# Spectral filter and low-rank mixer on one core: batch 0's spectra made twice by TensorE, one copy of the filters for its products, tables loaded from SP

## The chip, the core and the metric

The kernel runs on one core of one Trainium2 chip. The core has TensorE (PE; PEld is its weight load), VectorE (DVE), ScalarE (ACT), GpSimd (POOL) and SyncE (SP), each with an instruction queue of its own that it works through in order. PE writes to PSUM (eight banks of 2 KB in each of 128 partitions); DVE and ACT read PSUM and write SBUF; POOL works on SBUF. Transfers between memory and SBUF are issued from SP, ACT or POOL and share 16 DMA engines. The metric is the device time of one execution in microseconds (us), given as the median of three runs. The profile is taken from one further execution; its times are us from the start of its span.

## The reference

```python
batch, seq, dim = (8, 3136, 256)
n_freq = seq // 2 + 1
...
X = np.fft.rfft(x, axis=1)
F = (filt_r + 1j * filt_i)[None, :, :]
Y = X * F
y = np.fft.irfft(Y, n=x.shape[1], axis=1).astype(np.float32)
...
xt = y.transpose(0, 2, 1)
h = xt @ U @ V                      # U (3136, 32), V (32, 3136)
u = y + h.transpose(0, 2, 1)
ch = np.maximum(u @ w_ch1, 0.0) @ w_ch2     # 256 -> 1024 -> 256
out = (u + ch).astype(np.float32)
```

Inputs and output are float32; the kernel works in float16 with float32 sums in PSUM.

## The kernel before

The length 3136 is split as 64 x 49. A forward transform is then: a first stage of 64 points over q (matrix `w64`), a second stage of 49 points that takes in the twiddle factors (tables `t2`, one 98 x 128 matrix for each of 32 values of s), the product with the filter, and the two stages back (tables `g12`, then `s2` or `low`). A spectrum tile `px` holds, for two values of s, real parts of up to 49 frequencies in partitions 0 to 63 and imaginary parts in 64 to 127.

The filters lie in `ft`, in two halves of 32 x 256 columns. The first half holds the real parts in both partition halves; the second holds the imaginary parts in partitions 0 to 63 and, with the sign turned, in 64 to 127. So a product has two parts, `px` times the first half and `px` times the second, and the second needs `g12` with its partition halves exchanged (`swap_table`, POOL; for the first eight s a ready table `gs` is loaded). The highest frequency is put into `ft[64]` by a DVE copy from `nyq`.

**Batch 0** stays on the chip. `first_f1` makes the first stage from x (24 evacuations to `at`, half on DVE, half on ACT, with filler matmuls of `keep_on` between), `first_a` turns pieces of it with an identity matrix, and `first_mid` runs over 16 pairs of s (m): `forward` (px, one bank of tag "m"), `both_products` (one DVE instruction of 128 x 1024), `back` (8 matmuls into `pi`), and ACT's two copies into `et`. Four times, once for each eighth-of-64 part of the tables (`PARTS`), DVE first makes the second copies of the filters, `swap_real` and `swap_imag`. Fillers (`keep_in`) stand ahead of each px. Then 50 transposes give `e2`.

**Batches 1 to 7** go through memory between the stages: first-stage units (`f1_units`: one matmul of 512 columns, one copy on ACT or DVE, writes to `c1`; 13 units for a batch, from three pieces of x), `load_a`, products and the way back in `stream`, writes to `c2`, `load_e`. Batch 1 uses `both_products` and the exchanged tables, later batches `product` (three DVE instructions, one sum on POOL) and `g12`'s first half alone.

**The mixer** runs over groups of 4 x 128 columns: `make_u`, eight `mm1` with relu, `mm2` and the output. Its loop counts slots, about 48 to a batch; the work on the transforms of later batches is put into slots by hand (`put`, `run`). Unit k of batch 2's first stage is put at slot 4 + 1.1 k, which makes its first unit stand in slot 4 and the fifth, the first of the second piece of x, in slot 8.

**Queues.** POOL issues all loads of x, filters, tables, U, V and weights, in the order of the code: x of batch 0, filters and tables in four parts, x of batch 1 with `swap_table` between, V, w1, w2. Then, after `first_f1` in the code, x of batch 2 (first piece), the 14 copies of `v_order` that reorder V into `low`, x of batch 2 (second piece), and two copies that reorder w2. SP loads small constants at the start, then writes `c1` of batch 1.

PSUM's eight banks: tag "x" 1, "f" 1, "m" 4, "o" 2.

Of the kernel before, what the change touches and what calls it, by code (L numbers as in the profile page):

```python
# [13 lines left out]
SEQ = 3136  # L14
# [12 lines left out]
def _consts():  # L27
# [22 lines left out]
    for s in range(NS):  # L50
        for j in range(49):
# [15 lines left out]
            else:  # L67
# [3 lines left out]
                g[s, j, o:o + 49] = ei.real * (2 if f else 1)  # L71
                g[s, 64 + j, o:o + 49] = -ei.imag * 2

    t2[0, :, 64] = 0
    t2[0, 49:, 64] = (-1.0) ** r
    g[0, 64] = 0
    g[0, 64, 49:] = (-1.0) ** r
    g *= ESC / n
    gs = np.concatenate([g[:, 64:], g[:, :64]], 1)
# [5 lines left out]
            np.ascontiguousarray(g.reshape(4, 8, 128, 98).transpose(0, 2, 1, 3)).astype(f16),  # L85
            np.ascontiguousarray(gs[0:8].transpose(1, 0, 2)).astype(f16))
# [3 lines left out]
def kernel(  # L90
# [13 lines left out]
    w64_np, s2_np, idn_np, fold_np, wp_np, t2_np, g_np, gs_np = _consts()  # L104
# [7 lines left out]
    gs_d = nc.inline_tensor(gs_np, name="gsd")  # L112
# [8 lines left out]
    BUFS = {"x": 1, "f": 1, "m": 4, "o": 2}  # L121

    def bank(tag, name):
        return ps.tile([128, 512], F32, tag=tag, bufs=BUFS[tag], name=name)
# [48 lines left out]
    nyq = sb.tile([128, DM], F32, tag="ocho", bufs=1, name="nyq")  # L173
    PARTS = ((0, 8), (8, 16), (16, 24), (24, 32))
    for a, b in PARTS:
        for c in (0, NS * DM):
            nc.vector.memset(ft[32:64, c + a * DM:c + b * DM], 0.0)  # L177

    def load_table(k, a, b):

        dst, src, w = ((t2, t2_d, 128), (g12, g_d, 98))[k]
        n, p = (b - a) * w, dst.shape[0]
        nc.gpsimd.dma_start(dst[:, a * w:b * w],
                            bass.AP(tensor=src, offset=a // 8 * p * n, ap=[[n, p], [1, n]]))

    def swap_table(a, b):

        o = NS * 98
        for p, q in ((0, 64), (64, 0)):
            nc.gpsimd.tensor_copy(g12[p:p + 64, o + a * 98:o + b * 98],  # L190
                                  g12[q:q + 64, a * 98:b * 98])

    def load_filters(a, b):

        d = max(a, 1)
        for c, src in ((0, filt_r), (NS * DM, filt_i)):
            nc.gpsimd.dma_start(
                ft[0:24, c + a * DM:c + b * DM],
                bass.AP(tensor=src.tensor, offset=a * DM, ap=[[64 * DM, 24], [1, (b - a) * DM]]))
            nc.gpsimd.dma_start(  # L200
                ft[25:49, c + d * DM:c + b * DM].rearrange("p (k d) -> p k d", d=DM),
# [3 lines left out]
    def load_rest():  # L205

        for c, src in ((0, filt_r), (NS * DM, filt_i)):
            nc.gpsimd.dma_start(
                ft[25:49, c:c + DM],
                bass.AP(tensor=src.tensor, offset=32 * DM, ap=[[64 * DM, 24], [1, DM]]))  # L210
            nc.gpsimd.dma_start(
                ft[24:25, c:c + NS * DM],
                bass.AP(tensor=src.tensor, offset=24 * 64 * DM,
                        ap=[[NS * DM, 1], [1, NS * DM]]))
        nc.sync.dma_start(
            nyq[64:65, :],
            bass.AP(tensor=filt_r.tensor, offset=(SEQ // 2) * DM, ap=[[DM, 1], [1, DM]]))

    def swap_real(a, b):

        nc.vector.tensor_copy(ft[64:128, a * DM:b * DM], ft[0:64, a * DM:b * DM])

    def swap_imag(a, b):

        fb = NS * DM
        if a == 0:
            nc.vector.memset(ft[0:1, fb:fb + DM], 0.0)
        nc.vector.tensor_scalar_mul(ft[64:128, fb + a * DM:fb + b * DM],
                                    ft[0:64, fb + a * DM:fb + b * DM], -1.0)
# [9 lines left out]
    for k, part in enumerate(PARTS):  # L239
        if k:  # L240
            load_table(0, *part)
        load_filters(*part)
        if k == 0:
            load_table(0, *part)
        load_table(1, *part)
        if k == 0:
            nc.gpsimd.dma_start(g12[:, NS * 98:(NS + 8) * 98], gs_d.ap())
        if k > 1:
            swap_table(*PARTS[k - 1])
    load_x(1, 0)  # L250
    uq = sb.tile([128, NR * RANK], F16, tag="esb", bufs=2, name="uq")
    nc.vector.memset(uq[64:128, :], 0.0)
    nc.gpsimd.dma_start(uq[0:64, :], moe_U.rearrange("(q r) p -> q (r p)", q=NQ))
    load_x(1, 1)
    swap_table(*PARTS[3])
    load_x(1, 2)
    vqs = []
    for k in range(2):
        v = sb.tile([128, SEQ // 2], F16, tag="xt", bufs=5, name="vq")
        vqs.append(v)  # L260
        nc.gpsimd.dma_start(v[64:96, :], moe_V[:, k * (SEQ // 2):(k + 1) * (SEQ // 2)])
    w1 = cst.tile([128, 2 * 1024], F16)
    for i in range(4):
        nc.gpsimd.dma_start(
            w1[32 * i:32 * i + 32, :].rearrange("p (h c) -> p h c", h=2),
            bass.AP(tensor=moe_w_ch1.tensor, offset=moe_w_ch1.offset + i * 64 * 1024,
                    ap=[[1024, 32], [32 * 1024, 2], [1, 1024]]))
    w2 = cst.tile([128, 8 * DM], F16)
    w2n = sb.tile([128, 8 * DM], F16, tag="esb", bufs=2, name="w2n")
    nc.gpsimd.dma_start(w2n, moe_w_ch2.rearrange("(cc t) e -> cc (t e)", t=8))  # L270
# [6 lines left out]
    def v_order():  # L277

        for r in range(0, NR, 8):
# [8 lines left out]
            yield  # L288

# [66 lines left out]
    def first_f1():  # L356
        ne = 0
        xs = [st[0]["x"][c] for c in range(len(CH))]
        for r0 in range(0, NH - 1, 4):
            for dh in range(2):  # L360
                keep_on(4 if r0 < 16 else 0)
# [6 lines left out]
                for h in range(2):  # L368
                    dst = atv[:, dh, :, h * NH + r0:h * NH + r0 + 4]
                    src = pa.rearrange("p (r h k) -> p h k r", h=2, k=64)[:, h]  # L370
                    if ne % 2:
                        nc.vector.tensor_copy(dst, src)
                    else:
                        nc.scalar.copy(dst, src)
                    ne += 1
# [21 lines left out]

# [542 lines left out]
```

## Time and profile before

| | us |
|---|---|
| median of 3 runs | 523.87 |
| lowest, highest | 523.34, 524.46 |
| the profiled execution | 523.76 |
| its span | 522.0 |
| batch 0's 16 products on DVE, first start to last end | 19.98 to 44.16 |
| first `mm1` of the mixer (slot 0) | 53.61 |
| first px of batch 1 | 64.45 |

A line of the timeline has the start, the time from there to the end of the merged instructions, the engine, the source line, the operation, what it writes and reads with shapes, how many instructions are merged, and in square brackets the idle time of the engine before it and what ended it. A matmul's row is longer than the time it keeps PE, since matmuls are pipelined; the distance of starts tells the latter.

### The profile page before, as it was taken

The page shows a single profiled execution, that of the slowest core. Times are in us where ns is not written, and L with a number is a line of the kernel's source. Part 1 is how long each engine was busy: PE and PEld are TensorE (multiplying, and loading weights), DVE is VectorE, ACT ScalarE, POOL GpSimd, SP SyncE. Part 2 cuts the span into 40 slices and gives each one's busy share as a digit, 9 for nine tenths or more (in the row PEclk, how much of TensorE's full clock was granted, in tenths as well). Part 3 has the DMA queues.
Part 4 walks back from the last instruction along what each step waited for, and adds up shares of the span by engine and source line. Part 5 has one row for each costly group of instructions (what it writes and reads, how often), then busy time and mean ns, then how long its engine had stood idle before and what let it go on. Part 6 is the DMA issues. An engine that isn't in the chain of part 4 may idle for free.

```text
span 522.0 us, 11372 instructions
## 1 busy us (share of the span) xinstructions
PE 496.7 (95%) x3976; PEld 327.4 (63%) x3976; DVE 407.7 (78%) x585; ACT 377.5 (72%) x772; POOL 301.9 (58%) x430
## 2 busy tenths in 40 slices
PE   4878899999989999999999999999999999999997
PEld 3766477777656665666666666666666666555555
DVE  7897386677888888998998888988999877436654
ACT  2767757768778768887788878888777678665552
POOL 7798733445765757775777675965666564313001
PEclk9999999999999999999999999999999999999999
DMA  8989998978899798887898698888777575644325
GB/s 135 188 143 221 233 214 203 213 209 191 197 202 253 180 203 181 215 219 176 235 216 221 162 253 207 184 227 194 180 194 150 129 167 134 139 100 80 71 62 121
DMA packets 122571, 93.99 MB, mean 180 GB/s; under 512 B 58017, under 2 KB 104866, under 8 KB 122514
## 3 DMA queue, kind: packets, MB, share of 16 engines
q1 hardware_dynamic: 98986, 50.93, 39.1%
q0 software_dynamic: 20240, 40.60, 37.9%
q10 hardware_dynamic: 3288, 1.74, 1.3%
q8 instruction: 31, 0.51, 0.4%
q14 instruction: 26, 0.21, 0.1%
HBM read 56.25 MB, written 48.17 MB: 200 GB/s over the span
## 4 chain that ended last, share of the span: by engine, by line
PE 78%; DVE 9%; DMA 6%; POOL 3%; issue 2%; ACT 1%; ACTq 0%; SPq 0%; DVEq 0%; POOLq 0%
PE phh L712 28%; PE po L789 25%; PE px L516 5%; PE pi L552 5%; PE pu L637 4%; PE po L738 4%; DVE uv L537 4%; DMA xt<-in_x_dram 3%; PE pf L472 3%; PE ph L594 2%; DVE ft L177 1%; DVE uv L535 1%; DMA out_dram<-och 1%; DMA g<-gd 1%; DMA a<-c 1%
## 5 line engine op out<-in xcount | busy, mean ns | idle before, releaser
L720 ACT ACTIVATE h<-phh 128x512 f16<-128x512 f32 (+1 forms) x391 | 205.4, 578 | 68.6 <-PE phh L712 64.1
L712 PE MATMUL phh<-ut,w 128*128 128x512 f16 x768 | 197.5, 379 | 0.3 <-ACT h L720 0.3
L540 POOL TENSOR_TENSOR y<-uv 128x512 f16<-128x512 f16 x96 | 111.8, 1165 | 100.1 <-DVE uv L537 80.3
L789 PE MATMUL po<-h,w 128*128 128x512 f16 x656 | 168.5, 379 | 0.0
L712 PEld LDWEIGHTS <-w 128*128 128x128 f16 x832 | 114.2, 144 | 54.5 <-issue 0.9
L537 DVE TENSOR_TENSOR uv<-px,ft 64x512 f16<-64x512 f32 x192 | 132.1, 688 | 2.6
L807 POOL DMA_DIRECT2D out_dram<-och x148 | 85.9, 588 | 81.6 <-DVE och L799 38.9
L789 PEld LDWEIGHTS <-w 128*128 128x128 f16 x656 | 60.5, 98 | 57.8 <-issue 1.1
L535 DVE TENSOR_TENSOR uv<-px,ft 128x512 f16<-128x512 f32 x96 | 64.9, 676 | 35.2 <-PE px L516 33.0
L556 ACT CAST esb<-pi 98x512 f16<-98x512 f32 x112 | 65.9, 589 | 32.1 <-PE pi L552 28.2
L798 DVE TENSOR_TENSOR tt<-po,ut 128x512 f32<-128x512 f32 x82 | 56.7, 692 | 34.3 <-PE po L789 32.3
L799 DVE STREAM_TRANSPOSE och<-tt 128x512 f32<-128x512 f32 x82 | 58.4, 712 | 2.8
L516 PE MATMUL px<-a,t 98*128 98x256 f16 x256 | 49.1, 273 | 5.6 <-DVE uv L537 2.8
L478 ACT CAST asb<-pf 128x512 f16<-128x512 f32 (+1 forms) x80 | 46.1, 576 | 6.5 <-PE pf L472 3.8
L524 DVE TENSOR_TENSOR uv<-px,ft 128x1024 f16<-128x1024 f32 x32 | 38.0, 1219 | 11.7 <-PE px L516 11.2
L702 ACT CAST ut<-pu 128x512 f16<-128x512 f32 x82 | 44.8, 612 | 0.0
L516 PEld LDWEIGHTS <-t 98*128 98x128 f16 x256 | 22.7, 98 | 31.6 <-DVE uv L537 10.6
L552 PE MATMUL pi<-y,g 128*98 128x256 f16 x192 | 36.7, 272 | 0.1
L472 PE MATMUL pf<-xt,w 128*128 128x512 f16 (+1 forms) x91 | 33.2, 370 | 1.0 <-DMA xt<-in_x_dram 1.0
L738 PE MATMUL po<-w,h 128*128 128x256 f16 x256 | 33.2, 273 | 0.0
L552 PEld LDWEIGHTS <-g 128*98 128x98 f16 x256 | 29.6, 123 | 3.2 <-issue 0.8
L637 PEld LDWEIGHTS <-e 96*128 96x128 f16 x686 | 26.4, 98 | 7.2
(99 smaller groups left out, 420.0 us busy)
## 6 DMA issues: line engine op xcount, KB each, us to landing
xt<-in_x_dram POOLq DMA_DIRECT2D x46, 256.0 KB, 6.6
out_dram<-och SPq DMA_DIRECT2D x180, 64.0 KB
a<-c SPq DMA_DIRECT2D x28, 384.0 KB
e<-c SPq DMA_DIRECT2D x56, 192.0 KB
out_dram<-och POOLq DMA_DIRECT2D x148, 64.0 KB, 3.5
c<-esb SPq DMA_DIRECT2D x24, 384.0 KB
c<-asb POOLq DMA_DIRECT2D x30, 256.0 KB, 5.6
out_dram<-och POOLq DMA_DIRECT2D x12, 256.0 KB, 4.8
```

The source lines that it names most:

```text
L516: nc.tensor.matmul(px[:, sl * DM:(sl + 1) * DM], t2[:, s * 128:(s + 1) * 128], a2[:, (2 * ml + sl) * DM:(2 * ml + sl + 1) * DM], start=Tru ...
L535: nc.vector.tensor_mul(uv[:, 0:512], px[:, :], ft[:, a:a + 512])
L537: nc.vector.tensor_mul(uv[p:p + 64, 512:1024], px[q:q + 64, :], ft[q:q + 64, b:b + 512])
L540: nc.gpsimd.tensor_add(y, uv[:, 0:512], uv[:, 512:1024])
L552: nc.tensor.matmul(pi[0:98, sl * DM:(sl + 1) * DM], g12[:, g:g + 98], y[:, o:o + DM], start=(fi == 0), stop=(fi == nf - 1), skip_group_che ...
L556: nc.scalar.copy(split(esb[:, ml * 512:(ml + 1) * 512]), natural(pi[0:98, :]))
L712: nc.tensor.matmul(pm[:, 0:w], w1[:, dh * 1024:(dh + 1) * 1024].rearrange("p (c t) -> p t c", t=8)[:, t], ut[:, dh * w:(dh + 1) * w], star ...
L720: nc.scalar.activation(h[:, 0:w], pm[:, 0:w], RELU)
L789: nc.tensor.matmul(po[:, :], w2[:, t * DM + dh * 128:t * DM + (dh + 1) * 128], hs[gx, t][:, :], start=(t == 0), stop=(t == 7))
L798: nc.vector.tensor_add(tt, po[:, :], uts[gx][:, dh * 512:(dh + 1) * 512])
L799: nc.vector.transpose(och.rearrange("p (j h a) -> p h j a", h=2, a=32)[:, dh], tt.rearrange("p (j t) -> p j t", t=32))
L807: (nc.gpsimd if k and (b < nb - 1 or r0 > 12) else nc.sync).dma_start(dst, och[32 * i:32 * i + 32, k * 512:(k + 1) * 512] .rearrange("p (r ...
```

## The change

For batch 0, each px is made twice over: the real parts of two s, once in partitions 0 to 63 and once in 64 to 127 (first 512 columns, bank one), and likewise the imaginary parts (second bank). One DVE instruction multiplies all 1024 columns with one copy of the filters, in which partitions 0 to 63 hold real and 64 to 127 imaginary parts. The second copies that later batches need are made by 12 DVE copies (`spread_filters`): one between the middle and `prep_u`, one behind the transposes, ten in slots 0 to 9. The sign that stood in the filters moves into the exchanged table (POOL multiplies by -1) and, for batches 2 to 7, into a `scalar_tensor_tensor`. The highest frequency is handled as a 50th row of the first s, so `nyq`, `gs` and the fills of row 64 go.

Tables of parts 1 to 3 are loaded from SP, each pair behind a one-element copy (`mark`) of a tile that the queue thereby waits for. POOL's order becomes: x of batch 0, tables part 0, filters of parts 0 and 1, swap 0, filters 2, swap 1, filters 3, U, swap 2, batch 1's first two pieces of x, swap 3, its third, V, w1, w2, three steps of `v_order`, batch 2's first piece, the other four steps, w2's copies, batch 2's second piece. Batch 0's px tiles take two banks each, from a pool that uses the four banks of tag "m". In `first_f1` the evacuations go by tile and not by half tile, and the fillers are 4, 4, 4, 4, 12, 2, 2, 2; the fillers of the middle go. Batch 1's first-stage units move from the last four products to one there, one behind, and six among the transposes.

```diff
     for s in range(NS):
-        for j in range(49):
+        for j in range(49 if s else 50):
...
-    t2[0, :, 64] = 0
-    t2[0, 49:, 64] = (-1.0) ** r
-    g[0, 64] = 0
-    g[0, 64, 49:] = (-1.0) ** r
+    t2[0, :, (64, 113)] = 0
+    g[0, (64, 113)] = 0
...
+    @contextmanager
+    def four_banks(k):
+
+        with tc.tile_pool(name=f"pm{k}", bufs=2, space=bass.MemoryType.PSUM) as pool:
+            pm.append(pool)
+            yield
...
     for a, b in PARTS:
-        for c in (0, NS * DM):
-            nc.vector.memset(ft[32:64, c + a * DM:c + b * DM], 0.0)
+        for p in (32, 96):
+            nc.vector.memset(ft[p:p + 32, a * DM:b * DM], 0.0)
...
     def swap_table(a, b):
 
         o = NS * 98
-        for p, q in ((0, 64), (64, 0)):
-            nc.gpsimd.tensor_copy(g12[p:p + 64, o + a * 98:o + b * 98],
-                                  g12[q:q + 64, a * 98:b * 98])
+        nc.gpsimd.tensor_copy(g12[0:64, o + a * 98:o + b * 98], g12[64:128, a * 98:b * 98])
+        nc.gpsimd.tensor_scalar_mul(g12[64:128, o + a * 98:o + b * 98],
+                                    g12[0:64, a * 98:b * 98], -1.0)
...
+    def spread_filters():
+
+        for a, b in PARTS:
+            lo, hi = slice(a * DM, b * DM), slice((NS + a) * DM, (NS + b) * DM)
+            for dst, src in ((ft[0:64, hi], ft[64:128, lo]), (ft[64:128, hi], ft[64:128, lo]),
+                             (ft[64:128, lo], ft[0:64, lo])):
+                nc.vector.tensor_copy(dst, src)
+                yield
...
+    def tables_behind(k, ap):
+
+        nc.sync.dma_start(mark[:, k:k + 1], ap)
+        for t in range(2):
+            load_table(t, *PARTS[k], eng=nc.sync)
+
+    load_table(0, *PARTS[0])
+    load_filters(*PARTS[0])
+    load_table(1, *PARTS[0])
...
+    load_filters(*PARTS[1])
+    swap_table(*PARTS[0])
+    load_filters(*PARTS[2])
+
+    def loads(k):
+
+        swap_table(*PARTS[k])
+        if k == 1:
+            load_filters(*PARTS[3])
+            nc.gpsimd.dma_start(uq[0:64, :], moe_U.rearrange("(q r) p -> q (r p)", q=NQ))
+        elif k == 2:
+            load_x(1, 0)
+            load_x(1, 1)
+        else:
+            load_x(1, 2)
...
+    def load_weights():
...
+        for k, _ in enumerate(v_order()):
+            if k == 2:
+                load_x(2, 0)
+        for h in range(2):
+            nc.gpsimd.tensor_copy(split(w2)[:, :, h], natural(w2n)[:, :, h])
+        load_x(2, 1)
...
     def first_f1():
-                keep_on(4 if r0 < 16 else 0)
+                keep_on(4 if r0 < 8 else 12 if r0 == 8 and not dh else 2 if r0 < 16 else 0)
...
+            if r0 == 20:
+                tables_behind(1, atv[0:1, 0, 0, r0:r0 + 1])
...
     def first_a(m):
...
+        if ml == 0 and gi in (1, 2):
+            tables_behind(gi + 1, st[0]["a"][gi][0:1, 0:1])
+            loads(gi + 1)
+            if gi == 2:
+                load_weights()
...
     def first_mid(fill):
...
-        def ahead(m, keep=0):
-            return forward(m, st[0]["a"][m // 4], ("m",), keep)
-
-        pxs = [ahead(0), ahead(1)]
-        keep_on(8)
-        for m in range(NS // 2):
-            for k, part in enumerate(PARTS):
-                if k and 2 * m == part[0]:
-                    swap_real(*part)
-                    swap_imag(*part)
-            uv = both_products(m, pxs.pop(0))
-            if pend is not None:
-                back(*pend)
-            pend = (m, uv)
-            if m + 2 < NS // 2:
-                pxs.append(ahead(m + 2, 4 if m % 4 or not m else 14))
-            if m + 3 < NS // 2:
-                first_a(m + 3)
-            if m >= 12:
-                next(fill)
+        def ahead(m):
+
+            px = pm[-1].tile([128, 1024], F32, tag="px", bufs=2, name="px")
+            for fi in range(2):
+                for sl in range(2):
+                    s, o = 2 * m + sl, fi * 512 + sl * DM
+                    for q in (0, 64):
+                        nc.tensor.matmul(
+                            px[q:q + 64, o:o + DM], t2[:, s * 128 + fi * 64:s * 128 + fi * 64 + 64],
+                            st[0]["a"][m // 4][:, s % KG * DM:(s % KG + 1) * DM],
+                            start=True, stop=True, tile_position=(0, q), skip_group_check=True)
+            return px
+
+        with four_banks(1):
+            pxs = [ahead(0), ahead(1)]
+            for m in range(NS // 2):
+                uv = sb.tile([128, 1024], F16, tag="uv", bufs=3, name="uv")
+                fap = ft[:, 2 * m * DM:2 * (m + 1) * DM]
+                nc.vector.tensor_mul(
+                    uv.rearrange("p (f e) -> p f e", f=2),
+                    pxs.pop(0).rearrange("p (f e) -> p f e", f=2),
+                    bass.AP(tensor=fap.tensor, offset=fap.offset, ap=[fap.ap[0], [0, 2], [1, 512]]))
+                if pend is not None:
+                    back(*pend)
+                pend = (m, uv)
+                if m + 3 < NS // 2:
+                    first_a(m + 3)
+                if m + 2 < NS // 2:
+                    pxs.append(ahead(m + 2))
+                if m == NS // 2 - 1:
+                    next(fill)
+        later.enter_context(four_banks(2))
+        next(spread)
+        next(fill)
         prep_u()
         back(*pend)
...
-            if k4 in (1, 2, 3, 4):
+            if k4 < 6:
                 next(fill)
+            if k4 == 6:
+                next(spread)
...
     def product(m, px):
-        for p, q in ((0, 64), (64, 0)):
-            nc.vector.tensor_mul(uv[p:p + 64, 512:1024], px[q:q + 64, :],
-                                 ft[q:q + 64, b:b + 512])
+        nc.vector.scalar_tensor_tensor(uv[0:64, 512:1024], px[64:128, :], -1.0, ft[64:128, b:b + 512],
+                                       op0=mybir.AluOpType.mult, op1=mybir.AluOpType.mult)
+        nc.vector.tensor_mul(uv[64:128, 512:1024], px[0:64, :], ft[0:64, b:b + 512])
...
+    later = ctx.enter_context(ExitStack())
+    with four_banks(0):
+        first_f1()
+    loads(1)
     for m in range(3):
         first_a(m)
...
+    for k in range(10):
+        put(k, spread)
```

## The prediction, made before the changed kernel was run

> **What bounds the kernel now.** First the page's head and the busy table, then the busy time by stretches, whose first columns are the stretch, its length, and busy us (count) of PE, PEld, DVE, ACT and POOL.
>
> ```profile
> span 522.0 us, 11372 instructions
> PE 496.7 (95%) x3976; PEld 327.4 (63%) x3976; DVE 407.7 (78%) x585; ACT 377.5 (72%) x772; POOL 301.9 (58%) x430
> ...
> 20.00:44.00 24.00, 20.09 (x310) 17.34 (x307) 23.59 (x22) 16.38 (x47) 21.29 (x33) 1.00 0.92 161
> 53.60:65.00 11.40, 9.81 (x53) 5.54 (x53) 3.08 (x6) 9.30 (x19) 8.11 (x15) 1.00 1.05 242
> 110.00:480.00 370.00, 365.49 (x2806) 231.69 (x2805) 301.71 (x444) 288.32 (x585) 228.19 (x307) 1.00 0.79 186
> ```
>
> From 110 to 480 TensorE (PE) is busy 99%, so what the change moves before that reaches the end only as an earlier or later start of this stretch. In 20 to 44 (batch 0's middle) VectorE (DVE) is the full engine: 23.59 of 24.00. DVE in order of time (start, us, engine, line) shows the pattern, which repeats four times:
>
> ```profile
> 24.63 0.69 DVE L221 COPY ft<-ft 64x2048 f16<-64x2048 f16 x1
> 25.24 1.32 DVE L228 TENSOR_SCALAR ft<-ft 64x2048 f16<-64x2048 f16 x1
> 26.67 4.62 DVE L524 TENSOR_TENSOR uv<-px,ft 128x1024 f16<-128x1024 f32 x4
> ```
>
> Four products at 1.155 (4.62/4), then some 2.0 of filter copies. The 16th product ends at 44.16. Behind the middle, PE and GpSimd (POOL) in order of time show what comes last:
>
> ```profile
> 57.74 0.38 PE L472 MATMUL pf<-xt,w 128*128 128x512 f16 x1 [0.71 <-DMA xt<-in_x_dram]
> 62.78 0.39 PE L472 MATMUL pf<-xt,w 128*128 128x512 f16 x1 [0.27 <-DMA xt<-in_x_dram]
> ```
>
> ```profile
> 25.05 2.22 POOL L190 COPY g<-g 64x784 f16<-64x784 f16 x2 [0.69 <-DMA g<-gd]
> 35.84 1.71 POOL L190 COPY g<-g 64x784 f16<-64x784 f16 x2
> 47.50 8.56 POOL L284 COPY low<-vq 32x256 f16<-32x256 f16 x14
> 56.01 1.17 POOL L154 DMA_DIRECT2D xt<-in_x_dram  x2
> 57.22 2.01 POOL L837 COPY w<-w2n 128x1024 f16<-128x1024 f16 x2
> 102.10 1.15 POOL L540 TENSOR_TENSOR y<-uv 128x512 f16<-128x512 f16 x1 [2.29 <-DVE uv L537]
> ```
>
> The waits at 57.74 and 62.78 are for batch 2's first and second piece of x. The second is issued at 56.01 behind POOL's 8.56 of V reordering; its two transfers take 5.3 and 6.2 to land, the last at 62.74. So the second bound is POOL's queue: a shorter middle helps only as far as that piece lands earlier too.
>
> **The change, part by part.** Rows are us of the profiled execution.
>
> First stage: transfers of x are in the same places of POOL's queue, and the last piece of batch 0 lands at 15.2 as before. The fillers thin out: 0.107 each there (four L347 rows take 0.43). DVE and ACT each still evacuate 12 half tiles. PE's tiles from r=16 on still follow the third x piece (issued at 7.53, 7.1 to land: 14.6), so I take 0.4 less: the last ACT copy ends at 17.6 instead of 17.98. The thinner fillers have one more risk: PE's 128-column matmuls start 0.107 apart to 16.6 (L366) and 0.055 apart from 18.03 (L394). If that doubling came only after 19, each product until then would cost PE up to 1.2 more; PE is idle here for 2.0 at most (9.9 to 11.9) instead of 3.0, so I take 0.
>
> Middle, removed: four L221 (2.90), four L228 (4.02), L227 (0.17) and L828 (0.28) on DVE, 7.4 in all; on PE 86 filler matmuls at 0.055. Added on PE: px becomes eight 64-column matmuls of 256 in place of two of 128 columns. Line 594 already runs 32-column matmuls of 128 rows side by side: fours start 3 to 4 ns apart, and the fours follow at 0.11. Line 323 (64 columns) runs its two pairs in 0.35, where one 512-column matmul takes 0.21. So a pair costs 0.11, eight 0.44, against 0.22 for the old two. Going into and out of such a group costs about 0.1 each: L472 at 43.785 (0.21 long, as L712's four in 0.86) is followed by L323 at 44.095, and line 594's last start at 116.83 by L712 at 117.03. PE per product: eight L413 0.36, four L394 0.22, px 0.44, two changes 0.2, a semaphore 0.04: 1.26. The order matters: with two px buffers, px of product m+2 waits for product m, so PE's 1.26 is the period and not DVE's 1.155. First product: pt and ACT copies as at 18.03 to 19.3 before, less 0.4, plus 0.3 for the dearer px: 19.4, where before it was 19.98 (DVE's copies). End: 19.4 + 15 x 1.26 + 1.2 = 39.5, against 44.16: 4.7 gained.
>
> Behind the middle: six first-stage units of batch 1 stand among the transposes instead of four, two with fillers: 2 x (0.22 + 0.33) = 1.1, on PE, which is dense there (45.78 to 49.66). ACT's copies of two units come before its last et copies: +0.2. Left at slot 0 (L712, 53.61 before): 3.4, at 50.2.
>
> The spread (12 DVE copies of 64x2048, 0.69 each, up to 1.32 under a POOL copy) costs nothing where it stands: two in DVE gaps of 1.00 and 1.08 (before 46.44 and 51.31), ten in slots 0 to 9, where DVE is busy 3.08 of 11.40. Without that cover it would be 8.3 to 15.8 on DVE. Product for batches 2 to 7: 96 scalar_tensor_tensor replace 96 L537 (0.688). No such row exists; nearest are L537, L718 (0.692) and L798 (0.692), the far one L524 (1.22, twice the elements). I take 0.69, no change; the other end is 96 x 0.53 = 51 of DVE, whose idle time in 110 to 480 is 68. A gain is excluded, since all single-pass rows of 512 elements from PSUM stand at 0.67 or more.
>
> POOL's queue, the part that decides. Out: six table issues at 0.58 and one gs (0.55), which go to SP behind marks. SP's queue is idle from 3.4 to 44.8 before, so the marks hold back only the tables and then the c writes, whose first comes after 40. Their readers on PE have slack: t2 part 1 is marked at 16.4, lands near 21 and is read by px of product 4 at 23; parts 2 and 3 land near 27.5 and 32.5 for 28 and 33. In: four tensor_scalar_mul of 64x784. Near rows: L190 0.84 to 1.21; far row: L540, 1.165 for 512, so 1.78 for 784. I take 0.95, a pair 2.0. One setup instruction of POOL moves ahead of the first such mul; before it stands at 99.79, and L540 starts at 102.10, just after DVE released it at 101.95: 0 to 2.3. I take 0.
>
> The ledger: g part 0 lands at 18.8 (18.7 before); swap 0 to 20.8; four filter issues 2.3, to 23.1; swap 1 to 25.1; filters 27.4; U 27.9. Swap 2 needs g part 2 from SP: its mark follows ACT's copy of spectrum 4 (22.9), three SP issues at 0.45, then about 4 to land (a c write issued at 55.70 released its reader at 59.70): 28.2. Swap 2 to 30.2, batch 1's first two x pieces (four at 0.62) to 32.7. Swap 3 likewise: spectrum 8 copied at 27.9, table in at 33.2, to 35.2. Third x piece 2.5, V 1.0, w1 2.1, w2n 0.6: 41.4. V lands about 42.5. V reordering 8.56, batch 2's first x piece 1.2, w2 copies 2.0 (now ahead of the second piece): 54.3. Spread copies overlapping them: the L190 pair is 2.22 beside L228 and 1.71 alone; I add 0.5 (0 to 1.5). So the second piece is issued at 54.8 and lands 6.2 later, at 61.0.
>
> **Sum.** Free of waits PE would reach batch 2's fifth unit at 62.78 - 0.27 - 0.71 - 3.4 = 58.4; the piece arrives at 61.0. Gained there: 1.8. The 0.29 that px of batch 1 waits for its spectra at 64.45 falls away, since those follow the first stage (3.4 earlier): 2.1. The rest is PE's dense stretch. Span 522.0 - 2.1 = 519.9. The execution took 523.76, 1.76 around the span, so 521.7; the median (523.87) is 0.1 above it: **521.8**.
>
> **The rivals.** *More gain*: POOL is not the last; the piece lands by 58.4 and PE's own work sets slot 8. Gain 62.78 - 58.4 + 0.3 = 4.7: 519.2. For it: every gate but swap 2 and 3 is slack in the ledger; against it: the w2 copies now stand ahead of the piece. 0.14.
>
> *Nothing left*: POOL's copies are slowed by the spread at the upper end, or tables take 5 instead of 4 to land (g's rows: 4.4 to 5.3, by POOL). Issue at 56, landing at 62.3: 523.0 to 523.9. For it: L190 beside DVE. 0.22.
>
> *Slower, POOL's chain late*: setup and mul at their upper ends, 2.3 + 4 x 0.8 = 5.6, less 0.8 to 1.6 of slack in the gates. Place: swap 0; PE's first pi waits for it too. It decides from 2.0 behind the ledger; at 4.4 behind, the piece lands at 65.4: 2.7 later than before, less 0.3: 526.2. For it: both prices are unseen; against it: a copy on POOL is 0.84. 0.18. The Trainium skill (GPSIMD Engine Reference, Instruction dispatch) gives about 6 us, with no instruction of its own in the profile, for the first call after such a setup; as an estimate by that page the piece would land near 66 and the time be near 527. The trace disagrees: 2.3 at most.
>
> *The pairs don't run side by side* with 98 rows: px 0.88, PE 1.70 per product, middle to 46.1, 1.9 late, and the marks with it: about 527. Line 594 speaks against it. 0.05. *Dear scalar_tensor_tensor*: DVE over 90% busy in the dense stretch, 5 to 30 more: 0.05.
>
> **How the numbers follow.** The forecast holds 0.36, its own range 520.4 to 523.0 (0.5 to 1.2 of the ledger either way). About 0.2% (1.05 us) is what a measurement of this kernel can tell from no change. Faster: 0.14, most of 0.36 and a little of the second: 0.50. Same: 0.22. Slower: 0.28. The range reaches down to the larger gain and up to the late POOL chain: 518.9 to 526.2.
>
> **What would show it.** Right: DVE rows of the product 16 times between about 19.4 and 39.5 with no filter copies; px in pairs 0.11 apart; POOL's second x piece of batch 2 issued near 55 and PE waiting about 2.6 for it. Wrong: a gap before POOL's first mul, a mul of over 1.2, a scalar_tensor_tensor row far from 0.69, PE without a wait at that piece, or PE's late stretch not starting earlier by what the front gained.

## The result, and the profile after

| | before | after |
|---|---|---|
| median, us (4 runs each) | 523.66 | 530.68 |
| range | 523.34 to 524.46 | 530.28 to 531.2 |
| span of the profiled execution | 522.0 | 529.4 |
| batch 0's 16 products on DVE | 19.98 to 44.16 | 21.13 to 42.10 |
| first `mm1` (slot 0) | 53.61 | 53.42 |
| first px of batch 1 | 64.45 | 70.65 |

The ratio is 1.0132 with a 95% interval of 1.0115 to 1.0150: slower by 7, where 2 faster was forecast. The time is outside the range given (518.9 to 526.2).

The page's head and busy table of the changed kernel, then its busy time by stretches (columns as before: stretch, length, busy us of PE, PEld, DVE, ACT and POOL, granted clock of PE, DMA share, GB/s):

```profile
span 529.4 us, 11389 instructions
...
PE 502.1 (95%) x3980; PEld 327.7 (62%) x3980; DVE 412.4 (78%) x587; ACT 377.0 (71%) x772; POOL 307.3 (58%) x425
```

```profile
20.00:44.00 24.00, 22.60 (x316) 16.69 (x315) 20.94 (x21) 16.81 (x49) 23.15 (x29) 1.00 0.89 157
53.60:65.00 11.40, 6.94 (x28) 3.13 (x27) 7.60 (x9) 5.55 (x12) 9.32 (x12) 0.76 0.74 174
60.00:65.00 5.00, 3.64 (x14) 1.50 (x15) 1.36 (x2) 1.78 (x4) 2.98 (x4) 0.50 0.43 67
110.00:480.00 370.00, 364.62 (x2807) 232.42 (x2806) 302.33 (x444) 288.88 (x586) 229.86 (x306) 1.00 0.81 189
```

Read these from the bottom. From 110 to 480 PE is as full as before (364.62 against 365.49): the dense stretch has not changed, it starts later. In 20 to 44 the full engine is now POOL (23.15 of 24.00; 21.29 before), and DVE is relieved. In 53.6 to 65 PE is busy 6.94 where it was 9.81, and its clock is 0.76; from 60 to 65 it is 0.50. So the place of the loss is between slot 0 and the first px of batch 1. The timeline of PE there shows what PE waits for:

```profile
53.42 1.19 PE L744 MATMUL phh<-ut,w 128*128 128x512 f16 x4
...
61.36 0.58 PE L505 MATMUL pf<-xt,w 128*128 128x512 f16 x1 [4.46 <-DMA xt<-in_x_dram]
...
69.45 0.38 PE L505 MATMUL pf<-xt,w 128*128 128x512 f16 x1 [1.16 <-DMA xt<-in_x_dram]
70.65 0.38 PE L548 MATMUL px<-a,t 98*128 98x256 f16 x2
```

The two waits are the ones shown of before, for batch 2's first and second piece of x: 4.46 and 1.16, where they were 0.71 and 0.27. The timeline of POOL tells why the pieces come late (the first and last swap, then the end of its queue; a swap is here a copy and a multiplication):

```profile
19.20 0.83 POOL L191 COPY g<-g 64x784 f16<-64x784 f16 x1 [1.20 <-DMA g<-gd]
20.13 2.19 POOL L192 TENSOR_SCALAR g<-g 64x784 f16<-64x784 f16 x1
...
36.68 0.83 POOL L191 COPY g<-g 64x784 f16<-64x784 f16 x1 [0.42 <-DMA g<-gd]
37.59 2.17 POOL L192 TENSOR_SCALAR g<-g 64x784 f16<-64x784 f16 x1
...
47.31 4.55 POOL L280 COPY low<-vq 32x256 f16<-32x256 f16 x6
51.81 1.18 POOL L157 DMA_DIRECT2D xt<-in_x_dram  x2
52.96 6.36 POOL L280 COPY low<-vq 32x256 f16<-32x256 f16 x8
59.38 2.48 POOL L303 COPY w<-w2n 128x1024 f16<-128x1024 f16 x2
61.81 1.17 POOL L157 DMA_DIRECT2D xt<-in_x_dram  x2
```

A multiplication takes 2.17 to 2.19, a copy of the same shape 0.83. V's reordering, 14 copies in 8.56 before, takes 4.55 + 6.36 = 10.91. The second piece of x is issued at 61.81 (56.01 before), the first at 51.81. In the kernel before, the first stood ahead of V's reordering, in POOL's timeline:

```profile
46.26 1.19 POOL L154 DMA_DIRECT2D xt<-in_x_dram  x2
```

These are the parts of the 6.20 by which the first px of batch 1 comes later: slot 0 -0.19; waits for x 5.62 - 0.98 = +4.64; the wait of 0.29 for batch 1's spectra gone; and PE at half its clock. By windows of 1 us the clock is 0.73 in 59 to 60, 0.50 from 60 to 66, 0.86 in 66 to 67 and 1.00 after; PE works again from 61.36, and the clock is back at about 66.3, so PE loses about half of 4.9, 2.4 (an estimate). Together 6.6, near the 6.20. The rest of the 7.4 in the span (1.2) lies behind that px and was not followed.

In front of it, the middle: DVE's timeline has the products without filter copies between them, as it should, but they begin late:

```profile
21.13 3.61 DVE L456 TENSOR_TENSOR uv<-px,ft 128x1024 f16<-128x1024 f32 x3 [3.23 <-PE px L445]
25.60 14.94 DVE L456 TENSOR_TENSOR uv<-px,ft 128x1024 f16<-128x1024 f32 x12 [0.86 <-PE px L445]
40.88 1.23 DVE L456 TENSOR_TENSOR uv<-px,ft 128x1024 f16<-128x1024 f32 x1 [0.34 <-PE px L445]
```

DVE idles 3.23 for the first px: the pairs of 256 columns on PE start 0.21 apart there, the last of them at 25.24, and 0.106 apart in the next px.

### The profile page after: what moved, and what is told of

Read it like the earlier page. It is cut to its first block, busy times and chain, and to the rows that moved or that the text cites. A ratio compares the mean times of both kernels' runs of the same rounds, so it can differ in the third digit from the quotient of the medians.

```text
span 529.4 us, 11389 instructions
## 1 busy us (share of the span) xinstructions
PE 502.1 (95%) x3980; PEld 327.7 (62%) x3980; DVE 412.4 (78%) x587; ACT 377.0 (71%) x772; POOL 307.3 (58%) x425
## 3 DMA queue, kind: packets, MB, share of 16 engines
q1 hardware_dynamic: 99758, 52.13, 39.5%
## 4 chain that ended last, share of the span: by engine, by line
PE 78%; DMA 7%; DVE 6%; POOL 5%; issue 2%; ACT 1%; ACTq 0%; DVEq 0%; POOLq 0%
PE phh L744 28%; PE po L821 26%; DMA xt<-in_x_dram 6%; PE px L548 5%; PE pi L584 5%; PE po L770 4%; PE pu L669 4%; PE pf L505 3%; PE ph L626 2%; DVE uv L570 2%; DVE uv L568 2%; DVE uv L567 1%; POOL g L192 1%; POOL xt L157 1%; DMA g<-gd 1%
## 5 line engine op out<-in xcount | busy, mean ns | idle before, releaser
L568 DVE SCALAR_TENSOR_TENSOR uv<-px,ft 64x512 f16<-64x512 f32 x96 | 66.5, 693 | 1.3
L570 DVE TENSOR_TENSOR uv<-px,ft 64x512 f16<-64x512 f32 x96 | 65.6, 684 | 1.3
L831 DVE STREAM_TRANSPOSE och<-tt 128x512 f32<-128x512 f32 x82 | 58.4, 712 | 3.1 <-DMA out_dram<-och 0.3
L548 PE MATMUL px<-a,t 98*128 98x256 f16 x224 | 43.0, 273 | 4.2 <-DVE uv L570 3.3
L548 PEld LDWEIGHTS <-t 98*128 98x128 f16 x224 | 20.0, 98 | 28.9 <-DVE uv L570 10.8
L157 POOL DMA_DIRECT2D xt<-in_x_dram x50 | 30.1, 609 | 2.6 <-issue 1.0
```

The costliest lines, as they stand in the source:

```text
L548: nc.tensor.matmul(px[:, sl * DM:(sl + 1) * DM], t2[:, s * 128:(s + 1) * 128], a2[:, (2 * ml + sl) * DM:(2 * ml + sl + 1) * DM], start=Tru ...
L568: nc.vector.scalar_tensor_tensor(uv[0:64, 512:1024], px[64:128, :], -1.0, ft[64:128, b:b + 512], op0=mybir.AluOpType.mult, op1=mybir.AluOp ...
L570: nc.vector.tensor_mul(uv[64:128, 512:1024], px[0:64, :], ft[0:64, b:b + 512])
L831: nc.vector.transpose(och.rearrange("p (j h a) -> p h j a", h=2, a=32)[:, dh], tt.rearrange("p (j t) -> p j t", t=32))
```

## The experiments

Two theories stood at the start. A: POOL's queue is late, by the multiplications above all, and with it batch 2's x. B: PE's late rate (its matmuls start twice as far apart as later) at the start of the middle, or the tables, cost the time. The kernel before was run beside each set; its medians there were 524.36, 524.51, 524.26, 524.57 and 524.62.

| run | median | ratio to before, 95% | slot 0 | first px of batch 1 |
|---|---|---|---|---|
| e1 sign as copy | 530.83 | 1.010 to 1.014 | 55.74 | 71.48 |
| e2 tables ready | 525.63 | 0.999 to 1.0035 | 56.11 | 66.61 |
| e3 old fillers | 530.71 | 1.0099 to 1.0143 | 53.47 | 69.92 |
| e4 x first | 528.34 | 1.0062 to 1.012 | 51.75 | 68.03 |
| e5 spread later | 531.03 | 1.0073 to 1.015 | 53.13 | 66.87 |
| e6 sign as copy, tables early | 525.19 | 0.9981 to 1.0033 | 51.65 | 64.30 |
| e7 four edits | 524.35 | 0.9965 to 1.0023 | 54.10 | 66.55 |
| e8 before, x late | 531.96 | 1.0096 to 1.0178 | 53.09 | 71.29 |
| e9 tables early | 529.77 | 1.0079 to 1.0154 | 53.89 | 71.59 |
| e10 sign on DVE, tables early | 525.05 | 0.9993 to 1.0034 | 53.98 | 64.30 |
| e12 as e10, x first | 525.68 | 1.0011 to 1.0053 | 53.92 | 65.35 |
| e11 as e12, old fillers | 525.63 | 1.0002 to 1.0052 | 54.31 | 66.19 |
| e13 half table ready | 525.69 | 1.0014 to 1.0068 | 54.67 | 67.14 |
| e14 as e13, x first | 526.32 | 1.0028 to 1.0076 | 53.01 | 64.13 |
| e15 as e14, more fillers | 525.24 | 0.9994 to 1.0036 | 50.40 | 64.06 |
| e16 as e15, both pieces first | 528.67 | 1.0054 to 1.0113 | 53.79 | 69.64 |

The last two columns are each of one profiled execution. Those of e9, e13 and e16 lay 5.1, 2.7 and 2.5 above their medians, and the front differs by about 2 from one to the next, so only differences larger than that are read from them.

### e1: the multiplication as a copy

```diff
-        nc.gpsimd.tensor_scalar_mul(g12[64:128, o + a * 98:o + b * 98],
-                                    g12[0:64, a * 98:b * 98], -1.0)
+        nc.gpsimd.tensor_copy(g12[64:128, o + a * 98:o + b * 98],
+                              g12[0:64, a * 98:b * 98])
```

> The changed kernel with POOL's four multiplications by -1 as plain copies, so the second tables lack their sign (that part of the computation is left out). Theory A (POOL's queue decides: batch 2's second x piece is issued at 61.81 behind it): a copy of this shape takes 0.83 where the multiplication took 2.17; swaps 0 to 2 save 1.3 each, of which a part is lost waiting for the table of part 3 (it released swap 3 at 36.68), swap 3 saves 1.3 in full: the piece is issued 1.5 to 3 earlier and the time falls by as much, to 527.5 to 529. Theory B (TensorE's half rate until 24.5 and its waits in the middle decide): no change beyond 0.5.

No change in time: 530.83. The pairs on POOL took 1.7 each, as wanted, but the saving ended in a wait. POOL's timeline:

```profile
31.92 2.35 POOL L157 DMA_DIRECT2D xt<-in_x_dram  x4
40.57 0.84 POOL L191 COPY g<-g 64x784 f16<-64x784 f16 x1 [6.30 <-DMA g<-gd]
...
62.94 1.17 POOL L157 DMA_DIRECT2D xt<-in_x_dram  x2
```

POOL reached batch 1's x at 31.92, and SP issued the last g table at 32.89 behind its mark. Four transfers of x (256 KB each) had been asked before the table, and it came at 40.5; swap 3 waited 6.30. By the letter of the expectation this is theory B's case, but POOL's saving never reached the piece (issued at 62.94), so theory A was neither shown nor refuted: a second gate stood behind the first.

### e2: the second tables loaded ready made

```diff
     def swap_table(a, b):
...
-        nc.gpsimd.tensor_copy(g12[0:64, o + a * 98:o + b * 98], g12[64:128, a * 98:b * 98])
-        nc.gpsimd.tensor_scalar_mul(g12[64:128, o + a * 98:o + b * 98],
-                                    g12[0:64, a * 98:b * 98], -1.0)
+        n = (b - a) * 98
+        (nc.gpsimd if a == 0 else nc.sync).dma_start(
+            g12[:, o + a * 98:o + b * 98],
+            bass.AP(tensor=gs_d, offset=a // 8 * 128 * n, ap=[[n, 128], [1, n]]))
```

> The changed kernel with the second tables made on the host as constants and loaded (part 0 from POOL, parts 1 to 3 from SP behind the others), so POOL makes no swap at all: 12.0 of POOL's work goes, 0.6 MB of transfers more. Theory A: POOL then runs ahead until batch 2's first x piece waits for its buffer (batch 1's fourth unit, near 45.5); from there 6.4 of V copies, 2.5 of w2 copies: the second piece is issued near 56 in place of 61.81 and the time falls by 5 to 6, to 524.5 to 526. Theory B: by 1 at most (the 0.39 that TensorE waited for swap 3 and little else).

525.63, so 5 of the 7 are gone with the swaps off POOL: the second piece of x is issued at 57.63, and PE waits for no piece of batch 2's x. In exchange PE waits 0.86, 1.12 and 0.41 for tables, and slot 0 is at 56.11.

### e3: the old fillers

```diff
-                keep_on(4 if r0 < 8 else 12 if r0 == 8 and not dh else 2 if r0 < 16 else 0)
+                keep_on(4 if r0 < 16 else 0)
```

> The changed kernel with the first stage's fillers as before (4 ahead of each of the first eight tiles). Theory B: TensorE's starts reach 0.055 before the products as in the kernel before (at 18.03), the first product comes near 19.7 instead of 21.13 and the middle's last ends near 39.5 instead of 42.1, and the time falls by 2 to 3. Theory A: the middle gets shorter as well, but what it gains is waited for at batch 2's x pieces: the time falls by 0 to 1 (table 3 is asked for earlier, swap 3 waited 0.42 for it).

530.71. PE was at full rate at the first px here (pairs 0.106 apart, first product at 20.05), and the time did not move. But the middle did not get shorter either, as both theories had expected: its last product ended at 42.25 (42.10 in the changed kernel), since PE waited for POOL's multiplications, by PE's timeline:

```profile
27.54 0.46 PE L430 MATMUL pi<-g,uv 128*128 128x98 f16 x7 [0.41 <-POOL g L192]
...
33.60 0.46 PE L430 MATMUL pi<-g,uv 128*128 128x98 f16 x7 [0.95 <-POOL g L192]
36.26 0.63 PE L445 MATMUL px<-a,t 98*64 98x256 f16 x8 [0.73 <-DMA t<-t2d]
39.97 0.47 PE L430 MATMUL pi<-g,uv 128*128 128x98 f16 x7 [0.47 <-POOL g L192]
```

So this run alone does not clear theory B. That the late rate is not the cause of the 7 is shown by e10 below, which keeps these fillers and comes back to the time before. The waits for x were 3.57 and 1.16.

### e4: the second piece of x ahead of w2's copies

```diff
+        load_x(2, 1)
         for h in range(2):
             nc.gpsimd.tensor_copy(split(w2)[:, :, h], natural(w2n)[:, :, h])
-        load_x(2, 1)
```

> The changed kernel with batch 2's second x piece issued ahead of the two w2 copies (as in the kernel before) instead of behind them. Theory A: issued at 59.4 instead of 61.81, landed 2.5 earlier, time lower by 2 to 2.5: near 528.3. Theory B: no change.

528.34, 2.3 less, as theory A had it: the piece was issued at 57.29 (59.4 was expected) and the wait for it went; the wait for the first piece (4.54) stayed.

### e5: the filter copies later

```diff
     for k in range(10):
-        put(k, spread)
+        put(k + 6, spread)
```

> Changed kernel with the ten filter copies of slots 0 to 9 moved to slots 6 to 15, behind the reordering of V. If the DVE copies beside it stretch that reordering (10.9 us against 8.56 before), it takes 8.6 to 9.5 again, batch 2's second piece of x is issued 1.5 to 2.3 earlier (61.81 in the changed kernel), and the time is 528.5 to 529.3. If the stretch has another cause, the reordering stays near 10.9 and the time near 530.7.

The mechanism is there. POOL's timeline:

```profile
46.34 4.09 POOL L280 COPY low<-vq 32x256 f16<-32x256 f16 x6
...
51.67 4.50 POOL L280 COPY low<-vq 32x256 f16<-32x256 f16 x8
...
58.20 1.17 POOL L157 DMA_DIRECT2D xt<-in_x_dram  x2
```

V's reordering takes 8.59 in place of 10.91, and w2's copies 2.02 in place of 2.48: the stretch of POOL is the work of DVE's copies beside it. The piece is issued 3.6 earlier and its wait is gone; the first piece's (3.25) is not. The time, 531.03, missed the expectation: the gain was not seen in the median (the profiled execution, 529.13, was the fastest of six). The moved copies now stand beside batch 1's products: from 68 to 85 px waits six times for DVE, 3.09 together, where in the changed kernel it waits twice, 0.84. In the profiled execution that is about what is lost between the first px of batch 1 (3.8 earlier) and the end (2.1 earlier); it was not tried by itself.

### e6 and e9: marks one step earlier, with and without plain copies

```diff
-        if ml == 0 and gi in (1, 2):
+        if ml == 0 and gi < 2:
-            tables_behind(gi + 1, st[0]["a"][gi][0:1, 0:1])
+            tables_behind(gi + 2, st[0]["a"][gi][0:1, 0:1])
+        if ml == 0 and gi in (1, 2):
             loads(gi + 1)
```

e6 has this and e1's edit (so it too leaves out the sign), e9 this alone.

> The run with plain copies in place of the multiplications (sign left out, so the output is not the reference's), and SP's marks for table parts 2 and 3 moved one step earlier, behind spectra 0 and 4 in place of 4 and 8. If the multiplications cost the time and that run gained nothing only because swap 3 waited 6.30 for its table, POOL no longer waits there, the second piece of x is issued 3 to 4 earlier than 61.81 and the time is 526.5 to 528.5. If the multiplications do not matter, it stays at 529.5 to 531.5.

> Changed kernel with the marks of table parts 2 and 3 one step earlier and nothing else; with the run that has both this and plain copies (525.2) it tells the multiplications from the marks. If POOL's four multiplications of 2.17 hold the queue by themselves, swap 3's wait of 0.42 goes and little more: the second piece of x is issued at 60.5 to 61.5 and the time is 529.3 to 530.7. If the marks were what decided, the time is 525 to 527.

With e1 this makes a square: neither edit 530.7, copies alone 530.8, marks alone 529.8, both 525.2. Each alone does nearly nothing, both together 5.5. In e9 POOL has no wait left at the swaps and still issues the second piece at 61.18, so the multiplications fill the queue; in e1 the table was the next gate. In e6 neither holds, and the time is 1.3 below the range expected. POOL's timelines of e9 (last swap, second piece) and of e6 (the same):

```profile
37.40 2.17 POOL L192 TENSOR_SCALAR g<-g 64x784 f16<-64x784 f16 x1
...
61.18 1.17 POOL L157 DMA_DIRECT2D xt<-in_x_dram  x2
```

```profile
31.93 0.84 POOL L191 COPY g<-g 64x784 f16<-64x784 f16 x1
...
57.03 1.31 POOL L157 DMA_DIRECT2D xt<-in_x_dram  x2
```

A single undo would have acquitted the real cause.

### e10: the multiplication on DVE

```diff
-        nc.gpsimd.tensor_scalar_mul(g12[64:128, o + a * 98:o + b * 98],
-                                    g12[0:64, a * 98:b * 98], -1.0)
+    def sign_table(a, b):
+
+        o = NS * 98
+        nc.vector.tensor_scalar_mul(g12[64:128, o + a * 98:o + b * 98],
+                                    g12[0:64, a * 98:b * 98], -1.0)
...
+                if m % 4 == 0:
+                    sign_table(*PARTS[m // 4])
```

> The same marks, and the multiplication by -1 of each part moved from POOL to DVE, behind products 0, 4, 8 and 12 (here the output is the reference's). From DVE's TENSOR_SCALAR of 64x2048 at 1.0 to 1.3 one of 64x784 is 0.4 to 0.5, beside a PE period of 1.24 against DVE's 1.155. If POOL's multiplications are the loss, this comes where the plain copies came: 524.5 to 526. If DVE becomes the bound of the middle, slot 0 moves to 53 or later and the time is over 527.

525.05, as with plain copies and 4.7 below e9, which has the same marks and the multiplication on POOL; that settles the multiplication on POOL. DVE's timeline has the same instruction six times shorter:

```profile
22.46 0.36 DVE L196 TENSOR_SCALAR g<-g 64x784 f16<-64x784 f16 x1
...
39.01 0.36 DVE L196 TENSOR_SCALAR g<-g 64x784 f16<-64x784 f16 x1
```

PE's late rate was not touched here: the first product starts at 21.20 and slot 0 at 53.98, and yet the time is that of the kernel before.

### e8: the kernel before, with the piece late

```diff
-    load_x(2, 1)
     for h in range(2):
         nc.gpsimd.tensor_copy(split(w2)[:, :, h], natural(w2n)[:, :, h])
+    spare = cst.tile([64, 512], F16)
+    for k in range(7):
+        nc.gpsimd.tensor_copy(spare, g12[0:64, 0:512])
+    load_x(2, 1)
```

> The kernel before, with w2's copies and seven idle copies of 64x512 on POOL put ahead of batch 2's second piece of x, which is so issued some 5.5 to 6 later (56.01 before). If the late piece by itself is the loss, PE waits some 5.5 for it and the time is 528.5 to 530. If the changed kernel loses by other things and a late piece is made good later, the time is under 526.

531.96, 2 above the range expected: one late transfer by itself can make a loss as large as the whole one. (In the changed kernel it is shared between two pieces, and the first is waited for longest.) Issued at 61.80 as in the changed kernel, the second piece has PE waiting, by PE's timeline:

```profile
68.97 0.61 PE L472 MATMUL pf<-xt,w 128*128 128x512 f16 x1 [7.54 <-DMA xt<-in_x_dram]
```

PE's clock is 0.50 from 66 to 72 (windows of 1 and 2 us), as it was around the long wait of the changed kernel.

### e7, e12 and e11: several edits together

e7 is e2 with e3's fillers, e4's order and the early marks; e12 is e10 with e4's order; e11 is e12 with e3's fillers.

> Changed kernel with the second tables loaded ready made (no swaps on POOL), the old fillers of the first stage, the marks for parts 2 and 3 one step earlier, and batch 2's second piece of x ahead of w2's copies. If what stood between the gain of the middle and the end was POOL's queue, then the tables' landing and PE's late rate, PE waits neither for x nor (by more than 0.5) for tables, slot 0 starts at 50 to 52 and the time is 519.5 to 522.5, below the kernel before. If something else behind the middle takes the gain back, it stays at 523.5 to 526.

> As the last, and batch 2's second piece of x ahead of w2's copies. If the piece is still late there by about 2.3 (as with plain copies on POOL), it lands in time now: no wait of over 0.7 for x, and 522.5 to 524. If the front (slot 0 near 51.7) or batch 1's spectra set the start instead, 524.5 to 525.5.

> As the last, with the old fillers of the first stage, so that PE is at full rate from the first product on. With POOL out of the way the front should count now: the middle ends 1.5 to 2 earlier than with the new fillers, slot 0 starts at 49.7 to 50.5, and the time is 1 to 1.8 below the last run (521 to 522.5). If another bound (x, or batch 1's spectra by way of memory) stands there, it is within 0.5 of the last run.

None went below the kernel before: 524.35, 525.68 and 525.63 (e7 and e12 had been given 519.5 to 522.5 and 522.5 to 524 if POOL's queue were all, e11 521 to 522.5). e4's order is worth nothing once the multiplications are off POOL: in e10 the timeline of PE from 54 to 66 has only this wait for a transfer, and in e12 and e11 it is 1.05 and 1.50:

```profile
64.30 0.39 PE L555 MATMUL px<-a,t 98*128 98x256 f16 x2 [0.68 <-DMA a<-c]
```

Batch 1's spectra, which go through memory, are next. In e7 PE waits 0.70 for x and 1.93 for them; that the further tables it loads delay these transfers is likely, but was not tried. In e11 PE had half its rate until about 28 in spite of the old fillers, and so did not test the front.

### e13, e14, e15: half of the second table ready made

The half with the sign is loaded (100 KB for a part), POOL keeps the 0.83 copy; marks early. e14 adds e4's order, e15 more fillers.

```diff
-        nc.gpsimd.tensor_scalar_mul(g12[64:128, o + a * 98:o + b * 98],
-                                    g12[0:64, a * 98:b * 98], -1.0)
...
+    def load_half(a, b, eng):
+
+        n, o = (b - a) * 98, NS * 98
+        eng.dma_start(g12[64:128, o + a * 98:o + b * 98],
+                      bass.AP(tensor=gs_d, offset=a // 8 * 64 * n, ap=[[n, 64], [1, n]]))
...
-                keep_on(4 if r0 < 8 else 12 if r0 == 8 and not dh else 2 if r0 < 16 else 0)
+                keep_on(4 if r0 < 8 else 12 if r0 == 8 and not dh else 6)
```

> Marks one step earlier, POOL's multiplication gone: the half of the second table that carries the sign is loaded ready made (100 KB for a part, from SP; part 0 from POOL), the other half stays POOL's copy. The output is the reference's. If the multiplication's time on POOL is the loss and nothing else of it, this equals the run with plain copies (525.2): 524.5 to 526, with slot 0 near 51.7 and a wait of some 2 for batch 2's second piece of x. If the further loads delay the tables, PE waits for them and slot 0 is at 53 or later.

> As the last, with batch 2's second piece of x ahead of w2's copies. If what is left of the middle's gain (slot 0 some 2 earlier than in the kernel before) was lost only to that piece, it is 522 to 523.3, below the kernel before by 1 to 2. If batch 1's spectra, which go through memory behind the first-stage units, start the dense stretch, PE waits for them instead (0.7 to 1.5) and it is 524.3 to 525.5.

> As the last, with six fillers ahead of each tile of the first stage from the fifth tile on in place of two and none. If PE then has its full rate at the first product, the middle ends 1 to 2 earlier; if that counts at the end, the time is 0.7 to 1.5 below the last run; if the start of the dense stretch is set by batch 1's spectra or x, within 0.5 of it. If the fillers delay the first stage, later by up to 1.

e13 (525.69) has the time of e6, with its second piece issued at 59.26 in a profiled execution 2.7 above its median; e14 (526.32) gained nothing on it and lies above both of its ranges. By the intervals of the table e11 to e14 are slower than the kernel before, by 0.3 to 0.5%; e2, e6, e7, e10 and e15 cannot be told from it. e15 (525.24) is the instructive one. It is 1.1 below e14, as large as was expected if the front counts, but single executions of both scatter by more than that. Its middle is the one that was predicted. DVE's and PE's timelines:

```profile
19.58 14.30 DVE L465 TENSOR_TENSOR uv<-px,ft 128x1024 f16<-128x1024 f32 x12 [2.29 <-DMA ft<-in_filt_r_dram]
34.79 4.62 DVE L465 TENSOR_TENSOR uv<-px,ft 128x1024 f16<-128x1024 f32 x4 [0.91 <-DMA ft<-in_filt_i_dram]
```

```profile
50.40 1.20 PE L753 MATMUL phh<-ut,w 128*128 128x512 f16 x4
...
56.52 0.39 PE L514 MATMUL pf<-xt,w 128*128 128x512 f16 x1 [2.64 <-DMA xt<-in_x_dram]
...
64.06 0.38 PE L557 MATMUL px<-a,t 98*128 98x256 f16 x2 [0.36 <-DMA a<-c]
```

The products run from 19.58 to 39.41 and slot 0 starts at 50.40, 3.2 before the old one. Then PE waits 2.64 for batch 2's first piece of x (issued at 47.66, behind six of V's copies), works at half clock from about 58.2 to 61.6, and waits 0.36 for batch 1's spectra. The first px of batch 1 stands at 64.06, 0.39 before the old one. The front's gain turns into waiting and half clock.

### e16: the first piece of x ahead of V's reordering

```diff
-        for k, _ in enumerate(v_order()):
-            if k == 2:
-                load_x(2, 0)
+        load_x(2, 0)
+        for _ in v_order():
+            pass
```

> As the run with the stronger fillers, and batch 2's first piece of x ahead of all of V's reordering (there behind six of its 14 copies). PE's wait of 2.64 at 56.5 should fall to under 0.5. If that piece was the bound, px of batch 1 comes at 61 to 62 and the time is 521.5 to 523. If batch 1's spectra through memory are the next bound (they were asked from 57.6 to 61.6 and landed near 64), px of batch 1 stays at 63.5 to 64.5 with a wait of 1.5 to 3 for them, and the time is within 0.7 of the run without this edit (525.2).

528.67, 3.4 worse: an answer to another question. In the profiled execution slot 0 is 3.4 later than in e15 (53.79) and PE does not wait for the first piece at all. POOL waited 1.98 for the tile (PE still read batch 1's x from it), issued the piece at 47.16, only 0.5 earlier than e15, and did all of V's 10.87 behind it; the second piece was issued at 59.15 and PE waited 3.72. Which of the two next bounds alone would hold e15 where it is, and why batch 1's spectra came at 64 for slot 0 at 50.4, 53.0 and 54.0 alike (e15, e14, e10), stays open.

## Why the prediction was wrong, point by point

**The failed step: "I take 0.95" for `tensor_scalar_mul` on POOL, and the rest of POOL's ledger.** The instruction took 2.17, outside even the bounds given (0.84 to 1.78): a price per element from a copy or from L540's addition does not carry over to it. Against the ledger V's reordering began 4.8 late (47.3 for 42.5). The first swap began 0.4 late, and a pair of copy and multiplication took 3.04 to 3.08 where 2.0 was put, 4.2 in four; that is 4.6 of the 4.8. Then V took 10.91 where 8.56 plus 0.5 of contention was put (1.85), w2's copies 2.48 for 2.0. Together 7.1 with the 4.8; the piece was issued at 61.81 instead of 54.8. That the contention was DVE's copies is shown by e5. The Trainium skill (GPSIMD Engine Reference, Key points) says that POOL and DVE share their ways to SBUF and get in each other's way when DVE runs in a two-port mode; the trace agrees that each slows the other, with 8.59 against 10.91 on POOL and 0.69 against up to 1.2 for a copy on DVE, but does not show the mode.

**The rival that named it.** "Slower, POOL's chain late" was the mechanism, at 0.18. Its price (526.2) was too low: it let the chain be 4.4 late and it was 7.0, and it looked only at the second piece, while the first, behind the same queue, cost more (4.46 of 5.62). The setup in it cost nothing: the copy of swap 0 ends at 20.03, the first multiplication starts at 20.13. The gap of about 6 us that would follow from the Trainium skill (GPSIMD Engine Reference, Instruction dispatch) is not there.

**A term that no row was sought for: PE's clock after a long wait.** It is about 2.4 of the 7. The waits shown of before were under 0.8, so nothing there gave it.

**Front.** Right in its parts: px pairs 0.106 apart, 1.24 for a product at full rate (1.26), the first product and the end of the middle at 19.6 and 39.4 in e15 (19.4 and 39.5), slot 0 at 50.4 (50.2). The end agrees in part by luck: in e15 the products took 1.19 and 1.155 each, and waits of DVE for the filters, which the forecast did not have, made up for it. In the changed kernel itself the risk put at 0 came true: PE's rate doubled only at about 25.3. The first product came 1.7 and the end of the middle 2.6 later than forecast, and slot 0 gained 0.2, not 3.4. It did not decide the time (e10).

**Sum.** "Free of waits PE would reach batch 2's fifth unit at 58.4" held only for that unit's own piece; the first piece was put at nothing without a reason. By the ledger itself it goes out behind six of V's 14 copies, at about 46.2 (42.5 and 3.7), no earlier than the 46.26 of before, while PE would be there 3.4 earlier. e15 shows it: issued at 47.66, the piece holds PE 2.64 with slot 0 at 50.4. With POOL's delay removed the kernel is level with the one before (e6, e10, e15). That is the time of the rival "nothing left", but by other bounds than it named (the first piece of x, batch 1's spectra), so by luck.

**Right:** scalar_tensor_tensor at 0.693 (0.69); the spread hidden on DVE itself, though not on POOL; the pairs side by side; the dense stretch unchanged.

## What to carry to other kernels

An engine's time for one operation is no estimate of another's on the same shape: an unseen instruction on the queue that feeds the next stage deserves a range wide enough to change the forecast, or a run of its own. Removing one cause may show nothing when a second gate stands right behind it (e1 and e9 nothing, e6 5.5), so causes that could stand in a row are undone together and apart. And a shorter front is worth only what the transfers behind it can follow.

## What the runs showed of the hardware

- POOL's `tensor_scalar_mul` by a constant, 64x784 f16: 2.17; its copy of the same shape 0.83; the same multiplication on DVE 0.36.
- A wait of PE is dearer than its length, and in steps. Between 54 and 76 us of all these runs, by windows of 1 us, the granted clock stayed at 1.00 around waits of up to 1.93 (e7). It was 0.50 for about 3.4 us around each wait of 2.28 to 3.25 (e6, e15, e9 twice, e5), and for about 6.8 us around each of 3.54 to 7.54 (e1, e3, e16, the changed kernel, e4, e8); in the changed kernel and e8 PE had work in 4.9 and 3.6 of the 6.8. The Trainium skill (TensorE: Matmul & The Clock Gate, What's actually happening) gives about 3.4 us of idling for the fall and as much work for the return. The length of the steps agrees; the fall does not, since waits of 2.28 to 3.25 were enough here.
- The granted clock read 1.00 from 20 to 24 in the changed kernel, while matmuls of 128 columns started 0.107 apart, half the later rate (0.056 apart): at the start the distance of starts tells the rate, not that column. The moment of doubling moved between executions (in e11 later than in e3 with the same fillers).
